# Sliding-window attention plus SwiGLU on one core: one edge mask and the normalisation reordered, and the feed-forward loop run across its chunk boundaries

## The chip, the cores and the metric

The kernel runs on one NeuronCore of a Trainium2 chip, written in Bass with every engine's instruction list and every semaphore wait laid out by hand. Times are device microseconds of one execution, from first to last instruction with what lies around them. The kernel before took 840.69 us, the median of six runs (839.28 to 843.67).

## The reference

One input x of 2048 tokens by 576 features in bf16 is normalised, and two branches are added to it:

```
xn  = layernorm(x)
q, k, v = heads(xn @ wqkv)                     # 32 heads of 18
p   = softmax(q k^T * 18**-0.5, masked to 0 <= query - key < 256)
out = x + (p v) @ wo + (silu(xn @ w1) * (xn @ w3)) @ w2     # F = 4608
```

## The kernel before

Every operation goes through a recorder, `R.emit(engine, ...)`, which appends it to that engine's list; each list then runs strictly in the order in which it was recorded. Waits are on counting semaphores, one per engine, so a wait for a later instruction of an engine covers all earlier ones. Where an instruction stands in its engine's list is therefore the whole schedule.

**Prologue.** Layernorm, transposes to `xnT`, and the Q, K and V projections.

**Attention** (lines 484 to 648). Heads go in 8 groups `g` of four, and the 2048 keys in 16 blocks `i` of 128, which gives 128 steps. In a step the four heads' scores of key block `i` against query blocks `i` to `i+2` (L532, 128 by 384 per head; the last two steps of a group have only 256 and 128 columns) lie in the four banks of the PSUM tensor `STB`, one bank a head. Heads 0 and 1 are pair `p = 0`, heads 2 and 3 are pair `p = 1`. For each pair ScalarE takes the exponential of two banks in one instruction (L569); VectorE multiplies the diagonal block by a 0/1 mask (L574, "diagonal mask"); GpSimd zeroes part of the third block with an `affine_select` (L579, "edge mask"), which only the step two later reads; and the next step's scores for the pair are put in TensorE's list, since the exponential has freed the banks. Then TensorE's list gets 12 small matmuls of probabilities with V (L605, "PV"), which wait for all masks of the step, and VectorE's list a copy of the result to bf16 (L619). Last comes `pend_ufin`, the end of the step before: a transpose on TensorE (L627) and, on VectorE, the reciprocal of the row sums (L630) and the multiplication by it (L633), both reading the transpose.

So TensorE's order is: scores of step i+1 for pair 0, for pair 1, PV of i, transpose of i-1, scores of i+2. VectorE's order is: two diagonal masks of i, copy of i, reciprocal and multiplication of i-1, two diagonal masks of i+1.

**Output projection** (lines 660 to 741) multiplies by `wo` and adds x, into `xatt`.

**Feed-forward** (lines 743 to 878). Four chunks `ci` of 512 tokens, each with 36 units `fi` of 128 hidden features, 144 units in all. A unit is ten matmuls for gate and up (L784 to L794, into three rotating banks `GU`), a tanh and a scaled copy on ScalarE (L803, L806), one VectorE operation (`gs`, L810), one GpSimd product (`hT`, L816), and then the W2 stage: five matmuls (L829, L832) that accumulate over the 36 units of the chunk in five PSUM banks. The W2 stage of a unit is recorded after the gate and up matmuls of the next unit, so that the chain through ScalarE, VectorE and GpSimd lies beside TensorE's work. At the end of a chunk, however, the loop `while pending_w2` (L843) records the last W2 stage at once, ahead of the next chunk's first matmuls. The read-out of a finished chunk is recorded after the next chunk's first gate and up matmuls and ahead of that unit's own ScalarE and VectorE operations: a ScalarE copy of the 128 leftover columns (L851), four transposes (L856), and for each of four token blocks two VectorE additions, of 448 and of 128 columns (L865, L867), both waiting for the transposes, and the output DMA (L871). Weights stream in through three slots, refilled by SyncE after a slot's last W2 stage.

Of the kernel before, what the change touches and what calls it, by code (L numbers as in the profile page):

```python
# [6 lines left out]
ACT = mybir.ActivationFunctionType  # L7
ALU = mybir.AluOpType
# [96 lines left out]
def bass_parallel_sum__sliding_block__glu_gated_swiglu__prompt_kernel(  # L105
# [35 lines left out]
    with ExitStack() as es:  # L141
# [380 lines left out]
        pend_ufin = None  # L522

        def rec_scores(g, i, hh):
            j = g % 2
            nq = min(3, NT - i)
            N = 128 * nq
            q0 = i * 128
            wl = [tok_rep[g], pair_free[hh // 2]]
            if g == 0 and i == 0:  # L530
                wl.append(last_prologue_pe)
            tsc = R.emit(PE, lambda e, hh=hh, j=j, q0=q0, N=N: e.matmul(  # L532
                STB[:, hh, 0:N], kT[j][32 * hh:32 * hh + Dh, q0:q0 + 128], qT[j][32 * hh:32 * hh + Dh, q0:q0 + N],
                tile_position=(32 * hh, 0)),
                waits=wl, sig=s_pe)
            scores_tok[(g, i, hh)] = tsc

        first_sc_wait = [t for t in qk_ring_free if t is not None]
        for hh in range(4):
# [4 lines left out]
                STB[:, hh, 0:N], kT[0][32 * hh:32 * hh + Dh, 0:128], qT[0][32 * hh:32 * hh + Dh, 0:N],  # L544
# [8 lines left out]
        for g in range(G):  # L553
            j = g % 2
            for i in range(NT):
# [3 lines left out]
                for p in range(2):  # L559
# [18 lines left out]
                    if nq == 3:  # L578
                        tem = R.emit(POOL, lambda e, ps0=ps0: e.affine_select(  # L579
                            out=pview[:, ps0:ps0 + 2, 2, :], in_=pview[:, ps0:ps0 + 2, 2, :],  # L580
                            compare_op=ALU.is_ge, fill=0.0,
                            base=-1, pattern=[[0, 2], [-1, 128]], channel_multiplier=1),
                            waits=[ta], sig=s_pool)
                        last_pool_tok = tem
                        toks.append(tem)
# [6 lines left out]
                    step_masks += toks  # L592
                ub = UB[:, i % 2, :]
# [22 lines left out]
                last_pe_tok = pv_last  # L616
                uj = u_ctr % 2
# [7 lines left out]
                def ufin(uj=uj, td=td, i=i, g=g):  # L625
                    nonlocal utp_free, pb6_free
# [17 lines left out]
            if g + 2 < G:  # L644
                repack(g + 2)
        if pend_ufin is not None:
            pend_ufin()
            pend_ufin = None

# [100 lines left out]
        k_ctr = 0  # L750
        pending_w2 = []
# [10 lines left out]
        pending_readout = None  # L762
        for ci, (t0b, ntb) in enumerate(TCH):
            N = 128 * ntb
            c0 = t0b * 128
            for fi in range(NF):
                fc = fi // 4
                fl = fi % 4
                n = ci * NFC + fc
                t1, t3, t2, sl = tok_wfill[n]  # L770
                k = k_ctr
                k_ctr += 1
                mg = (2 * k) % 3
                mu = (2 * k + 1) % 3
                kj = k % 2
                k3 = k % 3
                wlg = [t1, tok_xnT_all, gu_bank_free[mg]]
                wlu = [t3, tok_xnT_all, gu_bank_free[mu]]
                if first_ffn:
                    extra = [attn_act_last, attn_dve_last, ep_dve_last, ep_pe_last]  # L780
                    wlg += extra
                    wlu += extra
                for kd in range(4):
                    R.emit(PE, lambda e, mg=mg, sl=sl, kd=kd, fl=fl, c0=c0, N=N: e.matmul(  # L784
                        GU[mg][:, 0:N], W1c[sl][:, kd, fl * 128:(fl + 1) * 128], xnT[:, kd, c0:c0 + N],
                        start=(kd == 0), stop=False), waits=wlg)
                for kd in range(4):
                    R.emit(PE, lambda e, mu=mu, sl=sl, kd=kd, fl=fl, c0=c0, N=N: e.matmul(  # L788
                        GU[mu][:, 0:N], W3c[sl][:, kd, fl * 128:(fl + 1) * 128], xnT[:, kd, c0:c0 + N],
                        start=(kd == 0), stop=False), waits=wlu)  # L790
                tg = R.emit(PE, lambda e, mg=mg, sl=sl, fl=fl, c0=c0, N=N: e.matmul(  # L791
                    GU[mg][:, 0:N], W1c[sl][0:64, 4, fl * 128:(fl + 1) * 128], xnT[0:64, 4, c0:c0 + N],
                    start=False, stop=True), waits=wlg, sig=s_pe)
                tu = R.emit(PE, lambda e, mu=mu, sl=sl, fl=fl, c0=c0, N=N: e.matmul(  # L794
                    GU[mu][:, 0:N], W3c[sl][64:128, 4, fl * 128:(fl + 1) * 128], xnT[64:128, 4, c0:c0 + N],
                    start=False, stop=True, tile_position=(64, 0)), waits=wlu, sig=s_pe)
                first_ffn = False
                if fi == 0 and pending_readout is not None:
                    pending_readout()
                    pending_readout = None  # L800
                if pending_w2:
                    pending_w2.pop(0)()
                ta = R.emit(ACTE, lambda e, kj=kj, mg=mg, N=N: e.activation(  # L803
                    th[kj][:, 0:N], GU[mg][:, 0:N], ACT.Tanh, scale=0.5),
                    waits=[tg, th_free[kj]], sig=s_act)
                tb_ = R.emit(ACTE, lambda e, kj=kj, mu=mu, N=N: e.activation(  # L806
                    us[kj][:, 0:N], GU[mu][:, 0:N], ACT.Copy, scale=0.5),
                    waits=[tu, us_free[kj]], sig=s_act)
                gu_bank_free[mu] = tb_
                tdg = R.emit(DVE, lambda e, kj=kj, mg=mg, N=N: e.scalar_tensor_tensor(  # L810
                    out=gs[kj][:, 0:N], in0=th[kj][:, 0:N], scalar=1.0, in1=GU[mg][:, 0:N],
                    op0=ALU.add, op1=ALU.mult),
                    waits=[ta, gs_free[kj]], sig=s_dve)
                gu_bank_free[mg] = tdg
                th_free[kj] = tdg
                to = R.emit(POOL, lambda e, k3=k3, kj=kj, N=N: e.tensor_tensor(  # L816
                    hT[k3][:, 0:N], gs[kj][:, 0:N], us[kj][:, 0:N], ALU.mult),
                    waits=[tdg, tb_, hT_free[k3]], sig=s_pool)
                us_free[kj] = to
                gs_free[kj] = to  # L820

                def w2_stage(fi=fi, k3=k3, sl=sl, fl=fl, ntb=ntb, to=to, t2=t2, ci=ci, N=N):
                    wl = [to, t2]
                    if fi == 0:
                        wl.append(out_free)
                        if ci == 0:
                            wl += [attn_dve_last, attn_pe_last, attn_act_last, ep_dve_last, ep_pe_last]
                    for tbi in range(ntb):
                        R.emit(PE, lambda e, tbi=tbi, k3=k3, sl=sl, fl=fl: e.matmul(  # L829
                            OUT448[tbi][:, 0:DR], hT[k3][:, tbi * 128:(tbi + 1) * 128], W2c[sl][:, fl, 0:DR],  # L830
                            start=(fi == 0), stop=(fi == NF - 1)), waits=wl)
                    last = R.emit(PE, lambda e, k3=k3, sl=sl, fl=fl, N=N: e.matmul(  # L832
                        PB7[:, 0:N], W2c[sl][:, fl, DR:576], hT[k3][:, 0:N],
                        start=(fi == 0), stop=(fi == NF - 1)), waits=wl, sig=s_pe)
                    hT_free[k3] = last
                    if fl == 3:
                        wslot_free[sl] = last
                        issue_next_fill()
                    return last

                pending_w2.append(w2_stage)

            while pending_w2:  # L843
                pending_w2.pop(0)()
            last_pe = hT_free[(k_ctr - 1) % 3]

            def readout(last_pe=last_pe, ntb=ntb, t0b=t0b, N=N):
                nonlocal o64_ctr, ofin_ctr, out_free
                ojt = o64_ctr % 2
                o64_ctr += 1  # L850
                tcp = R.emit(ACTE, lambda e, ojt=ojt, N=N: e.activation(  # L851
                    o128[ojt][:, 0:N], PB7[:, 0:N], ACT.Copy),
                    waits=[last_pe, o64_free[ojt]], sig=s_act)
                ttp = None
                for tbi in range(ntb):
                    ttp = R.emit(PE, lambda e, tbi=tbi, ojt=ojt: e.transpose(  # L856
                        o128t[:, tbi, :], o128[ojt][:, tbi * 128:(tbi + 1) * 128], ident[:]),
                        waits=[tcp, tok_ident], sig=(s_pe if tbi == ntb - 1 else None))
# [58 lines left out]
```

## Time and profile before

| what | value |
|---|---|
| median of six runs | 840.69 us (839.28 to 843.67) |
| the profiled execution: its time, its span | 840.42 us, 838.7 us |
| mean granted TensorE clock over the span | 0.852 |
| busy: TensorE, VectorE, ScalarE, GpSimd | 750.8, 325.0, 366.4, 273.5 us |
| attention, first score matmul to last normalisation | 93.3 to 323.1 us |
| feed-forward, first gate matmul to last W2 matmul | 362.3 to 832.5 us |

Busy time is the share in which an engine had an instruction running; TensorE's ends are modelled, and so its busy time is not a measure of how full it is. [...]

### The profile page before, as it was taken

Reading aid. Unit: us, or ns where it says so; the run is one execution under the profiler, and the core shown is the slowest. Engines: PE = TensorE matmul, PEld = TensorE weight load, DVE = VectorE, ACT = ScalarE, POOL = GpSimd, SP = SyncE. Lnnn points to the kernel's source line nnn. Section 1 sums busy time; section 2 is a strip of 40 time slices with the busy share of each in tenths; the row PEclk is TensorE's granted clock in tenths of the full one; section 3 lists DMA queues with packets and bytes.
Section 4 is the critical chain, followed back from the end, with each engine's and each line's share of the span. In section 5 each row is a group of like instructions: output and inputs, shape, how many; then the busy total and the mean of one; then the engine's idle time right before and its main releaser. Section 6 shows DMA issues by size and latency. Waiting matters only on the chain. (4 is left out here: it accounts for less than half of the span.)

```text
span 838.7 us, 13024 instructions
## 1 busy us (share of the span) xinstructions
PE 750.8 (90%) x4906; PEld 309.6 (37%) x4952; DVE 325.0 (39%) x974; ACT 366.4 (44%) x601; POOL 273.5 (33%) x410
## 2 busy tenths in 40 slices
PE   4999878777887788999999899999899999899996
PEld 2455323222222223434444334444344443344442
DVE  5564466666666664532222222222212222222222
ACT  1233678777877781023333333333233333233332
POOL 2111234333433340023333233333233333233332
PEclk9999755555555555999999999999999999999998
DMA  6110200110111006505445444454434534354320
GB/s 183 29 29 1 57 10 21 30 29 5 26 30 29 2 1 185 170 15 169 121 133 170 133 149 124 131 170 131 152 104 152 166 115 144 113 169 142 115 83 28
DMA packets 73917, 78.99 MB, mean 94 GB/s; under 512 B 4352, under 2 KB 72704, under 8 KB 73856
## 3 DMA queue, kind: packets, MB, share of 16 engines
q1 hardware_dynamic: 71552, 75.81, 30.4%
q10 hardware_dynamic: 2304, 2.36, 1.0%
q8 instruction: 39, 0.64, 0.3%
q14 instruction: 22, 0.18, 0.1%
HBM read 71.07 MB, written 2.36 MB: 88 GB/s over the span
## 5 line engine op out<-in xcount | busy, mean ns | idle before, releaser
L816 POOL TENSOR_TENSOR hT<-gs,us 128x512 bf16<-128x512 bf16 x144 | 165.7, 1151 | 348.2 <-DVE gs L810 348.2
L803 ACT ACTIVATE th<-stb 128x512 bf16<-128x512 f32 x144 | 86.0, 597 | 344.1 <-PE stb L794 344.1
L810 DVE SCALAR_TENSOR_TENSOR gs<-th,stb 128x512 bf16<-128x512 bf16 x144 | 99.0, 687 | 346.3 <-ACT th L803 346.3
L569 ACT ACTIVATE area<-stb 128x768 bf16<-128x768 f32 (+2 forms) x256 | 183.1, 768 | 42.5 <-PE stb L532 41.3
L788 PE MATMUL stb<-xnT,area 128*128 128x512 bf16 x555 | 144.3, 379 | 9.2 <-DVE gs L810 8.1
L784 PE MATMUL stb<-xnT,area 128*128 128x512 bf16 x573 | 148.5, 382 | 2.0 <-DVE xatt L728 1.0
L579 POOL TENSOR_SCALAR_AFFINE_SELECT area<-area 128x256 bf16<-128x256 bf16 x224 | 93.1, 416 | 151.4 <-ACT area L569 151.4
L605 PE MATMUL ub<-area 128*20 128x128 bf16 x1440 | 61.7, 301 | 45.4 <-DVE area L574 44.8
L532 PE MATMUL stb<-qT,kT 18*128 18x384 bf16 (+1 forms) x508 | 100.0, 475 | 1.4 <-ACT area L569 1.3
L806 ACT ACTIVATE us<-stb 128x512 bf16<-128x512 f32 x144 | 85.2, 592 | 0.0
L788 PEld LDWEIGHTS stb<-xnT,area 128*128 128x128 bf16 x576 | 56.1, 98 | 77.6 <-DVE gs L810 10.1
L784 PEld LDWEIGHTS stb<-xnT,area 128*128 128x128 bf16 x576 | 56.5, 99 | 65.6 <-issue 2.9
L574 DVE TENSOR_TENSOR area<-area,mask 128x256 bf16<-128x256 bf16 x256 | 78.0, 343 | 2.5 <-ACT area L569 2.5
L829 PE MATMUL ub<-area,hT 128*128 128x448 bf16 x288 | 78.7, 355 | 0.0
L619 DVE CAST uTsb<-ub 128x128 bf16<-128x128 f32 x128 | 37.4, 292 | 76.0 <-PE ub L605 76.0
L605 PEld LDWEIGHTS ub<-area 128*20 128x20 bf16 x1440 | 27.3, 109 | 93.5 <-DVE area L574 93.5
L829 PE MATMUL stb<-area,hT 128*128 128x448 bf16 x144 | 52.4, 364 | 6.4 <-POOL hT L816 6.4
L794 PE MATMUL stb<-xnT,area 64*128 64x512 bf16 x144 | 55.8, 388 | 0.0
L791 PE MATMUL stb<-xnT,area 64*128 64x512 bf16 x144 | 55.8, 388 | 0.0
L829 PE MATMUL pb<-area,hT 128*128 128x448 bf16 x144 | 51.2, 356 | 0.0
L832 PE MATMUL pb<-hT,area 128*128 128x512 bf16 x126 | 48.3, 383 | 0.0
L532 PEld LDWEIGHTS stb<-qT,kT 18*128 18x128 bf16 x508 | 24.8, 99 | 43.8 <-ACT area L569 29.1
(71 smaller groups left out, 533.5 us busy)
## 6 DMA issues: line engine op xcount, KB each, us to landing
area<-in_B_w_dram SPq DMA_DIRECT2D x72, 512.0 KB, 4.5
area<-in_B_w_dram SPq DMA_DIRECT2D x36, 576.0 KB, 6.1
area<-in_B_w_dram SPq DMA_DIRECT2D x72, 64.0 KB, 4.8
xin<-in_A_x_dram SPq DMA_DIRECT2D x16, 144.0 KB, 2.1
qT<-QTu SPq DMA_DIRECT2D x32, 72.0 KB
kT<-KTu SPq DMA_DIRECT2D x32, 72.0 KB
xres<-in_A_x_dram ACTq DMA_DIRECT2D x16, 144.0 KB, 2.3
out_dram<-ofin SPq DMA_DIRECT2D x16, 144.0 KB, 5.5
```

Source lines behind the costliest of these rows:

```text
L532: tsc = R.emit(PE, lambda e, hh=hh, j=j, q0=q0, N=N: e.matmul(STB[:, hh, 0:N], kT[j][32 * hh:32 * hh + Dh, q0:q0 + 128], qT[j][32 * hh:32 ...
L569: ta = R.emit(ACTE, lambda e, ps0=ps0, p=p, N=N: e.activation(pT3[:, ps0:ps0 + 2, 0:N], STB[:, 2 * p:2 * p + 2, 0:N], ACT.Exp, scale=scale ...
L574: tdm = R.emit(DVE, lambda e, ps0=ps0: e.tensor_tensor(pview[:, ps0:ps0 + 2, 0, :], pview[:, ps0:ps0 + 2, 0, :], mask_diag_b, ALU.mult), w ...
L579: tem = R.emit(POOL, lambda e, ps0=ps0: e.affine_select(out=pview[:, ps0:ps0 + 2, 2, :], in_=pview[:, ps0:ps0 + 2, 2, :], compare_op=ALU.i ...
L605: t_ = R.emit(PE, lambda e, hh=hh, ub=ub, kb=kb, g=g, ps=ps, jx=jx, start=start, stop=stop: e.matmul(ub[32 * hh:32 * hh + VW, 0:128], Vaug ...
L784: R.emit(PE, lambda e, mg=mg, sl=sl, kd=kd, fl=fl, c0=c0, N=N: e.matmul(GU[mg][:, 0:N], W1c[sl][:, kd, fl * 128:(fl + 1) * 128], xnT[:, kd ...
L788: R.emit(PE, lambda e, mu=mu, sl=sl, kd=kd, fl=fl, c0=c0, N=N: e.matmul(GU[mu][:, 0:N], W3c[sl][:, kd, fl * 128:(fl + 1) * 128], xnT[:, kd ...
L803: ta = R.emit(ACTE, lambda e, kj=kj, mg=mg, N=N: e.activation(th[kj][:, 0:N], GU[mg][:, 0:N], ACT.Tanh, scale=0.5), waits=[tg, th_free[kj] ...
L806: tb_ = R.emit(ACTE, lambda e, kj=kj, mu=mu, N=N: e.activation(us[kj][:, 0:N], GU[mu][:, 0:N], ACT.Copy, scale=0.5), waits=[tu, us_free[kj ...
L810: tdg = R.emit(DVE, lambda e, kj=kj, mg=mg, N=N: e.scalar_tensor_tensor(out=gs[kj][:, 0:N], in0=th[kj][:, 0:N], scalar=1.0, in1=GU[mg][:, ...
L816: to = R.emit(POOL, lambda e, k3=k3, kj=kj, N=N: e.tensor_tensor(hT[k3][:, 0:N], gs[kj][:, 0:N], us[kj][:, 0:N], ALU.mult), waits=[tdg, tb ...
L829: R.emit(PE, lambda e, tbi=tbi, k3=k3, sl=sl, fl=fl: e.matmul(OUT448[tbi][:, 0:DR], hT[k3][:, tbi * 128:(tbi + 1) * 128], W2c[sl][:, fl, 0 ...
```

## The change

Four edits, in attention and in the feed-forward loop.

1. Pair 0 now uses banks 2 and 3 of `STB`, and pair 1 banks 0 and 1.
2. Pair 1's edge mask is a VectorE multiplication by the mask (as the diagonal mask is), recorded after the step's PV and no longer among what that PV waits for; the later PVs that read the block wait for it. Pair 0's stays on GpSimd.
3. The end of a step is cut in two. The transpose stays where it was; the reciprocal and the multiplication (`norm`) are recorded one step later, after that step's diagonal masks and before its PV.
4. The feed-forward loop runs over all 144 units in one sequence. The last W2 stage of a chunk comes after the next chunk's first gate and up matmuls, as every other W2 stage does, and the read-out after that unit's own ScalarE, VectorE and GpSimd operations. In the read-out the four 448-column additions come first and wait only for the W2 stage, and the four 128-column additions follow them and wait for the transposes.

```diff
-                STB[:, hh, 0:N], kT[j]...
+                STB[:, (hh + 2) % 4, 0:N], kT[j]...
...
-                        pT3[:, ps0:ps0 + 2, 0:N], STB[:, 2 * p:2 * p + 2, 0:N], ACT.Exp, scale=scale),
+                        pT3[:, ps0:ps0 + 2, 0:N], STB[:, 2 - 2 * p:4 - 2 * p, 0:N], ACT.Exp, scale=scale),
...
                     if nq == 3:
-                        tem = R.emit(POOL, lambda e, ps0=ps0: e.affine_select(
...
+                        if p == 0:
+                            tem = R.emit(POOL, lambda e, ps0=ps0: e.affine_select(
...
+                        else:
+                            late_edge = (ps0, ta)
...
                     step_masks += toks
+                if pend_norm is not None:
+                    pend_norm()
+                    pend_norm = None
...
                 last_pe_tok = pv_last
+                if nq == 3:
+                    ps0, ta = late_edge
+                    tem = R.emit(DVE, lambda e, ps0=ps0: e.tensor_tensor(
+                        pview[:, ps0:ps0 + 2, 2, :], pview[:, ps0:ps0 + 2, 2, :], mask_edge_b, ALU.mult),
+                        waits=[ta], sig=s_dve)
+                    for hh in (2, 3):
+                        mask_tok[(g, i, hh)] = mask_tok[(g, i, hh)] + [tem]
...
                     uT_free[uj] = tp
+                    pend_norm = lambda: norm(tp, uj, i, g)
+
+                def norm(tp, uj, i, g):
+                    nonlocal utp_free, pb6_free
                     tr = R.emit(DVE, lambda e: e.reciprocal(
```

The feed-forward loop after the change, with what did not change cut out:

```
for k, (ci, fi) in enumerate(units):
    ...                                  # ten gate and up matmuls
    last_w2 = None
    if prev is not None:
        last_w2 = rec_w2(prev)           # five W2 matmuls of the unit before
    ...                                  # tanh, copy, gs, hT of this unit
    if prev is not None and fi == 0:
        pci = prev[7]
        rec_readout(last_w2, TCH[pci][1], TCH[pci][0], 128 * TCH[pci][1])
    prev = (fi, k3, sl, fl, ntb, to, t2, ci, N)
last_w2 = rec_w2(prev)
rec_readout(last_w2, TCH[-1][1], TCH[-1][0], 128 * TCH[-1][1])
```

## Rows read from the trace of the kernel before

**Rows 1.** Busy time by stretch (us, instructions), granted clock, DMA share, GB/s.

```profile
200.00:250.00 50.00, 39.82 (x454) 14.25 (x452) 32.63 (x142) 40.17 (x57) 20.11 (x49) 0.50 0.10 25
602.00:604.00 2.00, 2.00 (x8) 0.83 (x7) 0.69 (x1) 1.09 (x2) 0.55 (x1) 0.50 0.77 270
```

**Rows 2.** Timeline of one attention step: start, length, engine, line; idle before, releaser.

```profile
98.50 1.51 ACT L569 ACTIVATE area<-stb 128x768 bf16<-128x768 f32 x2 [0.33 <-PE stb L532]
99.04 0.50 PE L605 MATMUL ub<-area 128*20 128x128 bf16 x12 [0.32 <-DVE area L574]
...
99.48 0.29 PE L627 MATMUL pb<-ident,uTsb 128*128 128x128 bf16 x1
99.59 0.29 DVE L619 CAST uTsb<-ub 128x128 bf16<-128x128 f32 x1 [0.61 <-PE ub L605]
...
99.70 0.87 PE L532 MATMUL stb<-qT,kT 18*128 18x384 bf16 x4
99.80 0.18 DVE L630 RECIPROCAL rden<-pb 128x4 f32<-128x4 bf16 x1
100.02 0.23 DVE L633 TENSOR_TENSOR O_all<-pb,rden 128x72 bf16<-128x72 bf16 x1
...
100.08 0.41 POOL L579 TENSOR_SCALAR_AFFINE_SELECT area<-area 128x256 bf16<-128x256 bf16 x1 [0.29 <-ACT area L569]
100.17 0.66 DVE L574 TENSOR_TENSOR area<-area,mask 128x256 bf16<-128x256 bf16 x2
100.26 1.51 ACT L569 ACTIVATE area<-stb 128x768 bf16<-128x768 f32 x2 [0.26 <-PE stb L532]
...
100.88 0.50 PE L605 MATMUL ub<-area 128*20 128x128 bf16 x12 [0.32 <-DVE area L574]
```

**Rows 3.** Timeline of ScalarE: the first and the last two tanh.

```profile
364.55 0.60 ACT L803 ACTIVATE th<-stb 128x512 bf16<-128x512 f32 x1 [45.17 <-PE stb L794]
...
825.57 0.60 ACT L803 ACTIVATE th<-stb 128x512 bf16<-128x512 f32 x1 [2.04 <-PE stb L794]
...
828.70 0.60 ACT L803 ACTIVATE th<-stb 128x512 bf16<-128x512 f32 x1 [2.04 <-PE stb L794]
```

**Rows 4.** Timeline across the last chunk boundary.

```profile
712.36 0.36 PE L829 MATMUL stb<-area,hT 128*128 128x448 bf16 x1 [1.77 <-POOL hT L816]
...
713.34 1.03 PE L784 MATMUL stb<-xnT,area 128*128 128x512 bf16 x4
...
713.54 0.60 ACT L851 ACTIVATE o<-pb 128x512 bf16<-128x512 f32 x1 [2.70 <-PE pb L832]
...
715.49 0.40 PE L856 MATMUL pb<-ident,o 128*128 128x128 bf16 x4
...
715.72 1.03 PE L784 MATMUL stb<-xnT,area 128*128 128x512 bf16 x4
...
715.92 0.62 DVE L865 TENSOR_TENSOR ofin<-stb,xatt 128x448 bf16<-128x448 f32 x1 [4.84 <-PE pb L856]
...
716.46 0.21 DVE L867 TENSOR_TENSOR ofin<-pb,xatt 128x128 bf16<-128x128 bf16 x1
716.59 0.62 DVE L865 TENSOR_TENSOR ofin<-ub,xatt 128x448 bf16<-128x448 f32 x1
...
719.32 1.04 PE L788 MATMUL stb<-xnT,area 128*128 128x512 bf16 x4 [2.57 <-DVE gs L810]
```

**Rows 5.** Timeline: exponentials back to back; masks without GpSimd beside them.

```profile
93.72 4.45 ACT L569 ACTIVATE area<-stb 128x768 bf16<-128x768 f32 x6
...
318.84 0.48 DVE L574 TENSOR_TENSOR area<-area,mask 128x256 bf16<-128x256 bf16 x2
```

**Rows 6.** Diagonal masks at 150 to 250 us: least, median and greatest ns.

```profile
L574 DVE TENSOR_TENSOR area<-area,mask x114: 277/283/492, 150.1 to 249.8; 128x256 bf16<-128x256 bf16 x114
```

**Rows 7.** Timeline of the end, and of the first four input DMAs.

```profile
831.30 0.36 PE L829 MATMUL stb<-area,hT 128*128 128x448 bf16 x1 [1.56 <-POOL hT L816]
...
834.36 2.32 SPq L871 DMA_DIRECT2D out_dram<-ofin  x4
...
0.79 1.81 SPq L264 DMA_DIRECT2D xin<-in_A_x_dram  x4
```

More of the change, by code (lines that the diff above doesn't have):

```diff
@@ L532, in rec_scores @@
             tsc = R.emit(PE, lambda e, hh=hh, j=j, q0=q0, N=N: e.matmul(
-                STB[:, hh, 0:N], kT[j][32 * hh:32 * hh + Dh, q0:q0 + 128], qT[j][32 * hh:32 * hh + Dh, q0:q0 + N],
+                STB[:, (hh + 2) % 4, 0:N], kT[j][32 * hh:32 * hh + Dh, q0:q0 + 128], qT[j][32 * hh:32 * hh + Dh, q0:q0 + N],
                 tile_position=(32 * hh, 0)),
@@ L578, in bass_parallel_sum__sliding_block__glu_gated_swiglu__prompt_kernel @@
                     if nq == 3:
-                        tem = R.emit(POOL, lambda e, ps0=ps0: e.affine_select(
[L580 to L585, printed above, removed]
+                        if p == 0:
+                            tem = R.emit(POOL, lambda e, ps0=ps0: e.affine_select(
+                                out=pview[:, ps0:ps0 + 2, 2, :], in_=pview[:, ps0:ps0 + 2, 2, :],
+                                compare_op=ALU.is_ge, fill=0.0,
+                                base=-1, pattern=[[0, 2], [-1, 128]], channel_multiplier=1),
+                                waits=[ta], sig=s_pool)
+                            last_pool_tok = tem
+                            toks.append(tem)
+                        else:
+                            late_edge = (ps0, ta)
                     for hh in (2 * p, 2 * p + 1):
@@ L592, in bass_parallel_sum__sliding_block__glu_gated_swiglu__prompt_kernel @@
                     step_masks += toks
+                if pend_norm is not None:
+                    pend_norm()
+                    pend_norm = None
                 ub = UB[:, i % 2, :]
@@ L625, in ufin @@
                 def ufin(uj=uj, td=td, i=i, g=g):
-                    nonlocal utp_free, pb6_free
+                    nonlocal pend_norm
                     tp = R.emit(PE, lambda e: e.transpose(utp, uT_sb[uj][:], ident[:]),
@@ L645, in bass_parallel_sum__sliding_block__glu_gated_swiglu__prompt_kernel @@
                 repack(g + 2)
+        if pend_norm is not None:
+            pend_norm()
         if pend_ufin is not None:
@@ L648, in bass_parallel_sum__sliding_block__glu_gated_swiglu__prompt_kernel @@
             pend_ufin = None
+            pend_norm()
         attn_dve_last = tok_O[(G - 1, NT - 1)]
@@ L749, in bass_parallel_sum__sliding_block__glu_gated_swiglu__prompt_kernel @@
         ofin_ctr = 0
-        k_ctr = 0
-        pending_w2 = []
         o64_ctr = 0
@@ L761, in bass_parallel_sum__sliding_block__glu_gated_swiglu__prompt_kernel, with rec_w2 @@
         first_ffn = True
-        pending_readout = None
-        for ci, (t0b, ntb) in enumerate(TCH):
+        units = [(ci, fi) for ci in range(len(TCH)) for fi in range(NF)]
+        prev = None
+        def rec_w2(info):
+            (fi, k3, sl, fl, ntb, to, t2, ci, N) = info
+            wl = [to, t2]
+            if fi == 0:
+                wl.append(out_free)
+                if ci == 0:
+                    wl += [attn_dve_last, attn_pe_last, attn_act_last, ep_dve_last, ep_pe_last]
+            for tbi in range(ntb):
+                R.emit(PE, lambda e, tbi=tbi: e.matmul(
+                    OUT448[tbi][:, 0:DR], hT[k3][:, tbi * 128:(tbi + 1) * 128], W2c[sl][:, fl, 0:DR],
+                    start=(fi == 0), stop=(fi == NF - 1)), waits=wl)
+            last = R.emit(PE, lambda e: e.matmul(
+                PB7[:, 0:N], W2c[sl][:, fl, DR:576], hT[k3][:, 0:N],
+                start=(fi == 0), stop=(fi == NF - 1)), waits=wl, sig=s_pe)
+            hT_free[k3] = last
+            if fl == 3:
+                wslot_free[sl] = last
+                issue_next_fill()
+            return last
@@ new lines, in rec_readout @@
+        def rec_readout(last_pe, ntb, t0b, N):
+            nonlocal o64_ctr, ofin_ctr, out_free
+            ojt = o64_ctr % 2
+            o64_ctr += 1
+            tcp = R.emit(ACTE, lambda e: e.activation(
+                o128[ojt][:, 0:N], PB7[:, 0:N], ACT.Copy),
+                waits=[last_pe, o64_free[ojt]], sig=s_act)
+            ttp = None
+            for tbi in range(ntb):
+                ttp = R.emit(PE, lambda e, tbi=tbi: e.transpose(
+                    o128t[:, tbi, :], o128[ojt][:, tbi * 128:(tbi + 1) * 128], ident[:]),
+                    waits=[tcp, tok_ident], sig=(s_pe if tbi == ntb - 1 else None))
+            o64_free[ojt] = ttp
+            ojs = []
+            for tbi in range(ntb):
+                oj = ofin_ctr % NOF
+                ofin_ctr += 1
+                ojs.append(oj)
+                tblk = t0b + tbi
+                R.emit(DVE, lambda e, oj=oj, tbi=tbi, tblk=tblk: e.tensor_tensor(
+                    ofin[oj][:, 0:DR], OUT448[tbi][:, 0:DR], xatt[:, tblk, 0:DR], ALU.add),
+                    waits=[last_pe, tok_xatt[tblk], (s_out[oj], s_out[oj].count)])
+            for tbi in range(ntb):
+                oj = ojs[tbi]
+                tblk = t0b + tbi
+                tdo = R.emit(DVE, lambda e, oj=oj, tbi=tbi, tblk=tblk: e.tensor_tensor(
+                    ofin[oj][:, DR:576], o128t[:, tbi, :], xatt[:, tblk, DR:576], ALU.add),
+                    waits=[ttp, tok_xatt[tblk]], sig=s_dve)
+                out_free = tdo
+                R.emit(SP, lambda e, oj=oj, tblk=tblk: e.dma_start(out2[tblk * 128:(tblk + 1) * 128, :], ofin[oj][:]),
+                       waits=[tdo], sig=s_out[oj], amount=16)
@@ L764, in bass_parallel_sum__sliding_block__glu_gated_swiglu__prompt_kernel @@
+        for k, (ci, fi) in enumerate(units):
+            t0b, ntb = TCH[ci]
             N = 128 * ntb
             c0 = t0b * 128
[L766 to L858, printed above, removed]
-                o64_free[ojt] = ttp
-                for tbi in range(ntb):
-                    oj = ofin_ctr % NOF
-                    ofin_ctr += 1
-                    tblk = t0b + tbi
-                    wl = [last_pe, ttp, tok_xatt[tblk], (s_out[oj], s_out[oj].count)]
-                    R.emit(DVE, lambda e, oj=oj, tbi=tbi, tblk=tblk: e.tensor_tensor(
-                        ofin[oj][:, 0:DR], OUT448[tbi][:, 0:DR], xatt[:, tblk, 0:DR], ALU.add), waits=wl)
-                    tdo = R.emit(DVE, lambda e, oj=oj, tbi=tbi, tblk=tblk: e.tensor_tensor(
-                        ofin[oj][:, DR:576], o128t[:, tbi, :], xatt[:, tblk, DR:576], ALU.add),
-                        waits=wl, sig=s_dve)
-                    out_free = tdo
-                    R.emit(SP, lambda e, oj=oj, tblk=tblk: e.dma_start(out2[tblk * 128:(tblk + 1) * 128, :], ofin[oj][:]),
-                           waits=[tdo], sig=s_out[oj], amount=16)
@@ L875, in bass_parallel_sum__sliding_block__glu_gated_swiglu__prompt_kernel @@
-            pending_readout = readout
-        if pending_readout is not None:
-            pending_readout()
-            pending_readout = None
+            fc = fi // 4
+            fl = fi % 4
+            n = ci * NFC + fc
+            t1, t3, t2, sl = tok_wfill[n]
+            mg = (2 * k) % 3
+            mu = (2 * k + 1) % 3
+            kj = k % 2
+            k3 = k % 3
+            wlg = [t1, tok_xnT_all, gu_bank_free[mg]]
+            wlu = [t3, tok_xnT_all, gu_bank_free[mu]]
+            if first_ffn:
+                extra = [attn_act_last, attn_dve_last, ep_dve_last, ep_pe_last]
+                wlg += extra
+                wlu += extra
@@ new lines, in bass_parallel_sum__sliding_block__glu_gated_swiglu__prompt_kernel @@
+            for kd in range(4):
+                R.emit(PE, lambda e, mg=mg, sl=sl, kd=kd, fl=fl, c0=c0, N=N: e.matmul(
+                    GU[mg][:, 0:N], W1c[sl][:, kd, fl * 128:(fl + 1) * 128], xnT[:, kd, c0:c0 + N],
+                    start=(kd == 0), stop=False), waits=wlg)
+            for kd in range(4):
+                R.emit(PE, lambda e, mu=mu, sl=sl, kd=kd, fl=fl, c0=c0, N=N: e.matmul(
+                    GU[mu][:, 0:N], W3c[sl][:, kd, fl * 128:(fl + 1) * 128], xnT[:, kd, c0:c0 + N],
+                    start=(kd == 0), stop=False), waits=wlu)
@@ new lines, in bass_parallel_sum__sliding_block__glu_gated_swiglu__prompt_kernel @@
+            tg = R.emit(PE, lambda e, mg=mg, sl=sl, fl=fl, c0=c0, N=N: e.matmul(
+                GU[mg][:, 0:N], W1c[sl][0:64, 4, fl * 128:(fl + 1) * 128], xnT[0:64, 4, c0:c0 + N],
+                start=False, stop=True), waits=wlg, sig=s_pe)
+            tu = R.emit(PE, lambda e, mu=mu, sl=sl, fl=fl, c0=c0, N=N: e.matmul(
+                GU[mu][:, 0:N], W3c[sl][64:128, 4, fl * 128:(fl + 1) * 128], xnT[64:128, 4, c0:c0 + N],
+                start=False, stop=True, tile_position=(64, 0)), waits=wlu, sig=s_pe)
@@ new lines, in bass_parallel_sum__sliding_block__glu_gated_swiglu__prompt_kernel @@
+            first_ffn = False
+            last_w2 = None
+            if prev is not None:
+                last_w2 = rec_w2(prev)
+            ta = R.emit(ACTE, lambda e, kj=kj, mg=mg, N=N: e.activation(
+                th[kj][:, 0:N], GU[mg][:, 0:N], ACT.Tanh, scale=0.5),
+                waits=[tg, th_free[kj]], sig=s_act)
+            tb_ = R.emit(ACTE, lambda e, kj=kj, mu=mu, N=N: e.activation(
+                us[kj][:, 0:N], GU[mu][:, 0:N], ACT.Copy, scale=0.5),
+                waits=[tu, us_free[kj]], sig=s_act)
@@ new lines, in bass_parallel_sum__sliding_block__glu_gated_swiglu__prompt_kernel @@
+            gu_bank_free[mu] = tb_
+            tdg = R.emit(DVE, lambda e, kj=kj, mg=mg, N=N: e.scalar_tensor_tensor(
+                out=gs[kj][:, 0:N], in0=th[kj][:, 0:N], scalar=1.0, in1=GU[mg][:, 0:N],
+                op0=ALU.add, op1=ALU.mult),
+                waits=[ta, gs_free[kj]], sig=s_dve)
+            gu_bank_free[mg] = tdg
+            th_free[kj] = tdg
+            to = R.emit(POOL, lambda e, k3=k3, kj=kj, N=N: e.tensor_tensor(
+                hT[k3][:, 0:N], gs[kj][:, 0:N], us[kj][:, 0:N], ALU.mult),
+                waits=[tdg, tb_, hT_free[k3]], sig=s_pool)
@@ L880, in bass_parallel_sum__sliding_block__glu_gated_swiglu__prompt_kernel @@
+            us_free[kj] = to
+            gs_free[kj] = to
+            if prev is not None and fi == 0:
[4 more added lines that the diff above has]
+        rec_readout(last_w2, TCH[-1][1], TCH[-1][0], 128 * TCH[-1][1])
         fin = [(so, so.count) for so in s_out]
```

2 lines of the change are left out of this document (1 added, 1 removed).

## The prediction

> **What bounds the kernel now.** I read the busy times by stretch first, then the timeline of one attention step, then the timeline across a chunk boundary. The reader is to see that the two halves have different limits.
>
> [...] What sets the step is a ring, and there are two that close at the same length. The first goes through VectorE: PV starts at 99.04, the copy of its result 0.55 later, the multiplication 0.43 after that, the diagonal masks 0.15 later, both done after 0.66, and the next PV 0.05 on, at 100.88 [rows 2]. That is 1.84; the exponentials of the same two steps start 1.76 apart, the step alternates, and the mean is 1.80. The second goes through ScalarE and takes two steps: the exponentials end at 98.50 + 1.51 = 100.01; the PV that needs them starts 0.87 later, the transpose 0.44 after PV, the scores 0.22 after the transpose, the exponentials 0.56 after the scores, and these last 1.51 [rows 2]. The sum, 3.60, is 1.80 a step. Both rings share the 0.87, in which the diagonal masks stand in VectorE's list behind the copy, the reciprocal and the multiplication of an older block. ScalarE and TensorE each sit idle for about 0.3 of every step on account of it [rows 2].
>
> In the feed-forward part the bound is TensorE: units follow each other at 828.70 - 825.57 = 3.13 [rows 3]. The 143 intervals from the first tanh to the last should take 143 x 3.13 = 447.6 and took 464.15, so 16.6 us are lost at the three chunk boundaries [rows 3]. At the one shown TensorE waits 1.77 for the last hidden block and then 2.57 because the VectorE operation that frees a bank stands behind eight additions [rows 4]. After such a boundary the granted clock falls to 0.50 for a short stretch [rows 1].
>
> **The change, part by part.**
>
> *Bank rotation.* The same waits on the same pairs with other bank numbers: no instruction more, no instruction moved, and TensorE writes one pair of banks while ScalarE reads the other, as before. I cost it at nothing, and see no reason for a gain or a loss.
>
> *Normalisation one step later, and pair 1's edge mask on VectorE.* These go together. VectorE's order becomes: masks of i, reciprocal and multiplication of i-2, edge mask of i, copy of i. The reciprocal and multiplication (starts 0.43 after the copy, 0.15 before the next operation [rows 2]) now run while PV runs. So the time from the end of the exponentials to PV shrinks to release, mask, release: 0.07 from ScalarE to the operation that waits for it (GpSimd's start at 100.08), 0.28 for a mask alone (two in 0.48, the second starting 0.20 after the first [rows 5]), 0.05 to PV: 0.40. TensorE has a floor of its own, since the scores of pair 1 stand ahead of PV and start when the exponentials end; the four score matmuls end by the model at 99.70 + 0.87 = 100.57, which is 0.56 after the exponentials [rows 2], but their tail overlaps what follows. The bounds are 0.40 and 0.56, and I take 0.44, nearer the mask's row, because the modelled end is late. The second ring is then 0.44 + 0.44 + 0.22 + 0.56 + 1.51 = 3.17, or 1.585 a step, a gain of 0.215; over 128 steps 27.5 us. At 0.40 it is 30 us, at 0.56 it is 20 us.
>
> What the ring leaves behind must fit. VectorE's share of a step is, by starts, two masks 0.40, reciprocal 0.22, multiplication 0.15, edge mask 0.20, copy 0.21: 1.2 of 1.585 [rows 2, 5]. The added mask is covered by PV's run: the copy could not start before PV's start + 0.55 anyway. The transpose of i-1 now waits for the multiplication of i-2, which stands behind the masks of i: 0.35 + 0.22 + 0.23 + 0.06 = 0.86 after the exponentials, against 0.44 + 0.44 = 0.88 for PV to clear TensorE. That wait is level with what it stands beside, and it is the next thing late. GpSimd loses a 0.41 operation a step that nobody will miss. ScalarE's floor is (4.45 - 1.51) / 4 = 0.735 an exponential, 1.47 a step [rows 5]: no longer far away.
>
> A mask's length is not one number: 277 to 492 ns with a median of 283 [rows 6], and the pair at 100.17 took 0.66 with GpSimd running beside it against 0.48 without [rows 2, 5]. [...]
>
> *The feed-forward loop.* At a boundary the two waits of 1.77 and 2.57 go [rows 4]: the last W2 stage has a unit's matmuls ahead of it, and the bank-freeing operation stands ahead of the additions. What is late next is TensorE itself: the transposes stand in its list behind W2 and wait for the ScalarE copy. The copy starts 1.18 after W2's first matmul (713.54 - 712.36), takes 0.60, and with 0.05 for the release the transposes start at 1.83; they hold TensorE 0.23 (715.49 to 715.72), so the next gate matmul starts at 2.06 where it would start at 0.98 (713.34 - 712.36) [rows 4]. The cost is 1.08 a boundary, 3.2 for three. Behind them the first W2 stage of the new chunk waits for all eight additions: four of 0.54 and four of 0.13 [rows 4], from 1.2 to 1.4 after W2 began to at most 4.1; TensorE gets there after ten more matmuls, 2.14 (713.34 to 715.48), at 4.20. No wait, with little to spare; if it slips, it costs up to 1 us a boundary. SyncE's output DMAs stand behind a refill issued earlier, as before. With one gap of about 0.85 in place of 1.77 and 2.57 I expect no fall of the clock. The gain is 16.6 - 3.2 = 13.4; bounds 10 and 14.
>
> *The end.* The last W2 stage still waits for its own chain. The 448-column additions can start 1.18 after it begins, at 832.5, and the last 128-column one ends near 835; but the four output DMAs are issued one after another, and four took 1.81 at the start of the kernel [rows 7]. From about 834.9 that ends at 836.7, where it ended before (834.36 + 2.32). I count 0, between -0.3 and +0.3.
>
> **Sum.** 840.4 (the profiled execution; the median of the runs is 0.3 above it) - 27.5 - 13.4 = 799.5 us. With the bounds of each part together: 796 to 811.
>
> **Rivals.**
> 1. *The wait moves to the transpose.* If the deferred multiplication comes late, the transpose holds up the scores and attention gains nothing. For that it must end 0.45 later than reckoned, since the transpose started 0.87 + 0.44 = 1.31 after the exponentials before. For it: it now stands behind two masks and is level already. Against: both masks at their greatest row, 0.49 each, add only 0.4. Time: 840.4 - 13.4 = 827. Half of it would give 813.
> [...]
> 3. *VectorE becomes the bound, and slower.* If its operations don't overlap and all three masks run at the greatest length, a step is 3 x 0.49 + 0.18 + 0.23 + 0.29 = 2.17 [rows 2, 6], 0.37 above now: 840.4 + 47 - 13.4 = 874. The kernel is slower from 1.80 + 13.4/128 = 1.90 a step on. Against: starts follow each other at 0.20 to 0.22 in the rows, and one GpSimd operation in place of two leaves less to collide with.
>
> **How the numbers follow.** Forecast 0.76, rival 1 in whole or half 0.10, rival 2 0.10, rival 3 0.04. The range 783 to 815 holds the forecast, most of rival 2 and the half case of rival 1. About 0.3%, 2.5 us, is what a measurement of this kernel can tell from no change. Slower is rival 3, 0.04; the same needs the gains of one half eaten by the other, 0.02; faster 0.94.
>
> **What would show it.** In the changed profile: exponentials of successive steps about 1.58 apart; PV starting 0.40 to 0.56 after the exponentials end, with the reciprocal and multiplication beside PV; the copy no longer ahead of waiting masks; ScalarE's idle time in attention under 0.1 a step. At the boundaries: one TensorE gap of about 0.85 that ScalarE's copy ends, none ended by GpSimd or by `gs`, and 464.15 - 13.4 = 451 us from first tanh to last. A step still at 1.80, or a granted clock above 0.50 in attention, makes the prediction wrong.

## The result

The changed kernel takes 800.32 us, the median of eight runs (799.32 to 804.25), against 840.54 for the kernel before: a ratio of 0.9526 (95% interval 0.9509 to 0.9543). The forecast was 799.5. The profiled execution took 799.7 us with a span of 797.9, so 40.8 us of span went. They can be placed by the starts of the stages:

| stage | before | after | gain |
|---|---|---|---|
| to the first score matmul | 93.31 | 93.72 | -0.4 |
| attention, to the end of the last normalisation | 93.31 to 323.08 | 93.72 to 296.79 | 26.7 |
| output projection and first unit, to the first tanh | to 364.55 | to 337.66 | 0.6 |
| first to last tanh | 464.15 | 450.01 | 14.1 |
| last tanh to the end | 10.0 | 10.2 | -0.2 |

Busy time of the changed kernel in the same 50 us of attention as in [rows 1] (columns: TensorE, its weight loads, VectorE, ScalarE, GpSimd, granted clock, DMA):

```profile
200.00:250.00 50.00, 47.26 (x520) 16.46 (x519) 41.79 (x188) 45.47 (x65) 11.47 (x29) 0.50 0.10 25
```

TensorE went from 39.82 to 47.26 busy, ScalarE from 40.17 to 45.47, GpSimd from 20.11 to 11.47, and the granted clock, a share of TensorE's full speed, stayed at 0.50. One attention step of the changed kernel, the rows that answer to [rows 2]:

```profile
199.66 0.80 ACT L570 ACTIVATE area<-stb 128x768 bf16<-128x768 f32 x1
...
200.20 0.58 DVE L575 TENSOR_TENSOR area<-area,mask 128x256 bf16<-128x256 bf16 x2
200.51 0.10 PEld L533 LDWEIGHTS stb<-qT,kT 18*128 18x128 bf16 x2 [0.32 <-ACT area L570]
200.66 3.02 ACT L570 ACTIVATE area<-stb 128x768 bf16<-128x768 f32 x4 [0.20 <-PE stb L533]
200.70 0.18 DVE L648 RECIPROCAL rden<-pb 128x4 f32<-128x4 bf16 x1
200.91 0.23 DVE L651 TENSOR_TENSOR O_all<-pb,rden 128x72 bf16<-128x72 bf16 x1
...
200.94 0.50 PE L612 MATMUL ub<-area 128*20 128x128 bf16 x12
201.06 0.28 DVE L626 TENSOR_TENSOR area<-area,mask 128x256 bf16<-128x256 bf16 x1
...
201.38 0.29 PE L641 MATMUL pb<-ident,uTsb 128*128 128x128 bf16 x1
201.50 0.29 DVE L633 CAST uTsb<-ub 128x128 bf16<-128x128 f32 x1 [0.16 <-PE ub L612]
...
201.60 1.13 PE L533 MATMUL stb<-qT,kT 18*128 18x384 bf16 x4
...
203.88 2.32 ACT L570 ACTIVATE area<-stb 128x768 bf16<-128x768 f32 x3 [0.20 <-PE stb L533]
```

Four exponentials now run back to back, 3.02 long, and the next four begin 3.22 after the first began: 1.61 a step in place of 1.80; ScalarE's one wait in the two steps is 0.20, which is 0.10 a step. The exponentials end at 199.66 + 0.80 = 200.46 and PV starts at 200.94, 0.48 later instead of 0.87. Reciprocal and multiplication lie beside PV, and the copy at 201.50 waits 0.16 for PV instead of 0.61. The masks are done at 200.78, before PV starts; what ends just ahead of PV is pair 1's scores, whose weights were loaded at 200.51.

The first and the last two tanh answer to [rows 3]:

```profile
337.66 0.60 ACT L872 ACTIVATE th<-stb 128x512 bf16<-128x512 f32 x1 [43.85 <-PE stb L865]
...
784.54 0.60 ACT L872 ACTIVATE th<-stb 128x512 bf16<-128x512 f32 x1 [2.04 <-PE stb L865]
...
787.67 0.60 ACT L872 ACTIVATE th<-stb 128x512 bf16<-128x512 f32 x1 [2.04 <-PE stb L865]
```

A unit still takes 3.13. The first chunk boundary, beside [rows 4]:

```profile
449.76 0.36 PE L792 MATMUL stb<-area,hT 128*128 128x448 bf16 x1
...
450.94 0.60 ACT L808 ACTIVATE o<-pb 128x512 bf16<-128x512 f32 x1
451.09 0.62 DVE L823 TENSOR_TENSOR ofin<-stb,xatt 128x448 bf16<-128x448 f32 x1
...
451.59 0.40 PE L813 MATMUL pb<-ident,o 128*128 128x128 bf16 x4 [0.69 <-ACT o L808]
451.83 1.03 PE L855 MATMUL stb<-xnT,area 128*128 128x512 bf16 x4
...
453.22 0.61 DVE L829 TENSOR_TENSOR ofin<-pb,xatt 128x128 bf16<-128x128 bf16 x4
...
453.98 0.36 PE L792 MATMUL stb<-area,hT 128*128 128x448 bf16 x1
```

The waits of 1.77 and 2.57 are gone. One is left, which ScalarE's copy ends, and the next gate matmul starts 2.07 after W2's first. The additions end at 453.83, 0.15 before TensorE wants the banks. At the end of the kernel, beside [rows 7]:

```profile
790.28 0.36 PE L792 MATMUL stb<-area,hT 128*128 128x448 bf16 x1 [1.56 <-POOL hT L885]
...
793.60 0.60 DVE L829 TENSOR_TENSOR ofin<-pb,xatt 128x128 bf16<-128x128 bf16 x4
793.84 1.82 SPq L833 DMA_DIRECT2D out_dram<-ofin  x4
```

The last four output DMAs are issued 1.82 long, from 3.56 to 5.38 after the last W2 stage began; before they ran from 3.06 to 5.38, each behind its own block's additions, of which the last ended 5.01 after that stage began (at 836.31). Now the last addition ends after 3.92, the issues follow each other, and nothing ends sooner.

### The profile page after: what moved, and what is told of

It reads as the page before. It is cut to its first block, busy times and chain, and to the rows that moved or that the text cites. A ratio compares the mean times of both kernels' runs of the same rounds, so it can differ in the third digit from the quotient of the medians.

```text
span 797.9 us, 13024 instructions
## 1 busy us (share of the span) xinstructions
PE 753.8 (94%) x4906; PEld 309.7 (39%) x4952; DVE 344.6 (43%) x1086; ACT 365.6 (46%) x601; POOL 226.9 (28%) x298
## 4 chain that ended last, share of the span: by engine, by line
PE 80%; ACT 12%; DVE 3%; DMA 3%; issue 2%; SPq 1%; POOL 0%; DVEq 0%; ACTq 0%
PE stb L855 16%; PE stb L859 15%; ACT area L570 11%; PE stb L533 7%; PE ub L792 7%; PE stb L862 6%; PE stb L792 5%; PE stb L380 4%; PE ub L612 4%; PE pb L792 3%; PE pb L795 3%; PE ub L339 2%; PE pb L641 2%; DMA xres<-in_A_x_dram 2%; PE ub L732 1%
## 5 line engine op out<-in xcount | busy, mean ns | idle before, releaser
L533 PE MATMUL stb<-qT,kT 18*128 18x384 bf16 (+1 forms) x508 | 114.5, 476 | 9.7 <-ACT area L570 3.1
L581 POOL TENSOR_SCALAR_AFFINE_SELECT area<-area 128x256 bf16<-128x256 bf16 x112 | 46.4, 414 | 171.9 <-ACT area L570 171.9
```

## The experiments

**The halves apart.** The attention edits alone, and the feed-forward loop alone:

```diff
 e1: attention of the changed kernel, feed-forward loop (L743 to L878) of the kernel before
 e2: attention of the kernel before, feed-forward loop of the changed kernel
```

> The attention edits with the feed-forward loop of before. Theory (the two halves have separate limits and their gains add): the attention part loses 26.7 us as in the changed kernel, the feed-forward part takes its 464 us as before, 814 us. Rival (the halves interact, for instance the earlier start of the weight stream costs or gives something later): the loss from before lies outside 25 to 29 us.

> The new feed-forward loop with the attention of before. Theory: first tanh to last tanh takes 450.0 us as in the changed kernel, against 464.2, and the rest is unchanged: 826.5 us. Rival (halves interact): outside 824.5 to 828.5.

The first took 817.05 us, ratio 0.97 (0.9674 to 0.9726), a gain of 24.3, just outside what was expected. Its profiled execution took 813.6, with 202.99 in attention and 464.06 from the first tanh to the last, which are the theory's numbers; the three timed runs took 817 at a granted clock of 0.862 against 0.866. Where those 3.4 us lie is open, since only one execution has a trace. The traces show two things that differ between executions. One is how often the clock falls from 1.00 to 0.50 at the old boundaries: at one of three in e3 (below), at two here and in the kernel before (there at 602 to 604 us [rows 1] and at 722 to 724), at three in e4, with 462.47, 464.06, 464.15 and 465.48 from the first tanh to the last, so a fall goes with about 1.5 us more, an estimate from these four. The other is when the clock comes back after attention (last section). The second took 825.86, ratio 0.9815 (0.9797 to 0.9834), with 450.02 between the tanh. The two gains, 24.3 and 15.5, add to 39.8; together the edits gave 40.2.

**The two attention edits apart**, each in the kernel before:

```diff
 e3 (late normalisation alone)
...
+                    pend_norm = lambda: norm(tp, uj, i, g)
 e4 (pair 1's edge mask alone)
-                        toks.append(tem)          # GpSimd, both pairs
...
+                        else:
+                            late_edge = (ps0, ta) # VectorE, after PV
...
+                    norm(tp, uj, i, g)            # at once, as before
```

> Only the late normalisation, all else of before; both edge masks stay on GpSimd and in what PV waits for. Theory (a step is the longer of two rings): the VectorE ring is opened, but PV now waits for GpSimd's mask of pair 1 and for a VectorE mask that collides with it, about 0.67 us after the exponentials in place of 0.87: 1.70 us a step, 828 us (824 to 832). Rival 1 (the order of the normalisation is the whole gain): 814. Rival 2 (relieving GpSimd is the whole gain): 840.

> Only pair 1's edge mask on VectorE, after PV; the normalisation stays directly behind the copy. Theory: the VectorE ring stays closed (PV, copy, reciprocal, multiplication, two masks) and gains only what the masks lose in length when GpSimd is not beside them, 0.04 to 0.14 us a step: 822 to 835, 829. Rival 1 (the order of the normalisation is the whole gain): 840. Rival 2 (relieving GpSimd is the whole gain): 814.

The late normalisation alone took 828.19 us, ratio 0.9848 (0.9824 to 0.9872). One of its steps:

```profile
211.73 3.02 ACT L570 ACTIVATE area<-stb 128x768 bf16<-128x768 f32 x4 [0.46 <-PE stb L533]
...
214.74 0.69 DVE L575 TENSOR_TENSOR area<-area,mask 128x256 bf16<-128x256 bf16 x2
214.82 0.47 POOL L581 TENSOR_SCALAR_AFFINE_SELECT area<-area 128x256 bf16<-128x256 bf16 x1 [0.30 <-ACT area L570]
...
215.20 3.02 ACT L570 ACTIVATE area<-stb 128x768 bf16<-128x768 f32 x4 [0.45 <-PE stb L533]
...
215.48 0.50 PE L610 MATMUL ub<-area 128*20 128x128 bf16 x12 [0.18 <-DVE area L575]
```

The exponentials end at 214.75, GpSimd starts its edge mask at once, the two VectorE masks take 0.69 beside it, and PV starts 0.73 after the exponentials. Four exponentials start 3.47 after the four before them, 1.73 a step. The edge mask alone took 825.17 us, ratio 0.9807 (0.9779 to 0.9835):

```profile
212.80 1.51 ACT L570 ACTIVATE area<-stb 128x768 bf16<-128x768 f32 x2 [0.15 <-PE stb L533]
...
213.24 0.50 PE L612 MATMUL ub<-area 128*20 128x128 bf16 x12
...
213.79 0.29 DVE L633 CAST uTsb<-ub 128x128 bf16<-128x128 f32 x1 [0.41 <-PE ub L612]
...
214.22 0.23 DVE L650 TENSOR_TENSOR O_all<-pb,rden 128x72 bf16<-128x72 bf16 x1
214.37 0.48 DVE L575 TENSOR_TENSOR area<-area,mask 128x256 bf16<-128x256 bf16 x2
...
214.91 0.50 PE L612 MATMUL ub<-area 128*20 128x128 bf16 x12
```

This is the ring of the kernel before, with the same 0.55, 0.43 and 0.15 in it [rows 2]. Only the pair of masks has shrunk, to 0.48, and PV follows PV after 1.67. That is 0.13 less than the mean of 1.80, and 0.13 x 128 = 16.6 us. PV starts 0.60 after the exponentials end at 214.31.

So neither edit is the whole gain. How far the two add is read from attention alone, because the runs' 13.1 and 16.2 also hold what differs in the feed-forward loop, where neither edit is. From the first score to the last normalisation the traces take 229.77 before, 217.49 with e3, 214.22 with e4 and 203.07 with both: 12.3 and 15.6, together 27.8, against 26.7. The gains add but for about 1 us, and two traces of the old attention (before and e2) differ by 0.4. Each edit takes its own part of the same stretch, the 0.87 from the exponentials to PV: 0.14 with the first, 0.27 with the second, 0.39 with both.

**What holds PV in the changed kernel.** Pair 1's diagonal mask is left out of the computation, and PV waits for the exponential in its place:

```diff
-                    tdm = R.emit(DVE, ... mask_diag_b, ALU.mult), waits=[ta], sig=s_dve)
+                    tdm = ta
+                    if p == 0:
+                        tdm = R.emit(DVE, ... mask_diag_b, ALU.mult), waits=[ta], sig=s_dve)
```

> The changed kernel without pair 1's diagonal mask (left out, so those probabilities are unmasked), PV waiting for the exponential itself. Theory (in the changed kernel PV is held by TensorE's own list, where pair 1's scores stand ahead of it): PV still starts about 0.46 us after the exponentials, step 1.60, 799 us (796 to 802). Rival (PV is held by the mask, 0.07 + 0.28 + 0.05): PV starts up to 0.35 earlier, ScalarE's floor of 1.47 to 1.51 decides, 785 to 789.

It took 798.83 us, ratio 0.9514 (0.9475 to 0.9552), no different from the changed kernel by its interval. A step of it, with the weight loads of pair 1's scores and of PV:

```profile
209.28 0.10 PEld L533 LDWEIGHTS stb<-qT,kT 18*128 18x128 bf16 x2 [0.35 <-ACT area L570]
...
209.72 0.50 PE L614 MATMUL ub<-area 128*20 128x128 bf16 x12
```

PV starts 0.44 after the scores' weights, as in the changed kernel (200.51 to 200.94, 0.43). In the wide steps the mask was not what held it; TensorE's own list was. At a group's end, where the scores are narrower, the mask does count: attention takes 200.96 in this trace against 203.07, and most of the 2.1 lies there.

**Scores ahead of the transpose.** In TensorE's list the transpose of an older block goes behind pair 0's next scores:

```diff
+                    if p == 0 and len(pend_list) >= 2:
+                        pend_list.pop(0)()        # transpose of i-1, behind the scores of i+2
...
-                if pend_ufin is not None:
-                    pend_ufin()
```

> The changed kernel with the transpose of an older block put behind pair 0's next scores in TensorE's list in place of ahead of them. Theory (the two-step ring through ScalarE decides, 0.47 + 0.44 + 0.22 + 0.57 + 1.51 = 3.21): without the 0.22 it is 2.99, and the floor is ScalarE's 1.47 to 1.51 or TensorE's 0.43 + 0.43 + 0.44 + 0.22 = 1.52 a step; 1.52 is 789 us (787 to 793). Rival (VectorE's list sets the step): 800.

It took 790.33 us, ratio 0.9402 (0.9369 to 0.9435). TensorE's list over one step:

```profile
219.78 0.50 PE L533 MATMUL stb<-qT,kT 18*128 18x384 bf16 x2
...
220.21 0.29 PE L640 MATMUL pb<-ident,uTsb 128*128 128x128 bf16 x1
...
220.42 0.50 PE L533 MATMUL stb<-qT,kT 18*128 18x384 bf16 x2
...
220.86 0.50 PE L614 MATMUL ub<-area 128*20 128x128 bf16 x12
...
221.29 0.50 PE L533 MATMUL stb<-qT,kT 18*128 18x384 bf16 x2
```

Busy time in 100 us of attention, columns as in the first such row:

```profile
150.00:250.00 100.00, 99.09 (x1097) 35.28 (x1093) 84.96 (x396) 96.49 (x135) 24.28 (x60) 0.50 0.11 26
```

Starts follow each other at 0.43, 0.21, 0.44 and 0.43, together 1.51 a step: TensorE's list at the clock that it is granted is now full, and ScalarE is 0.96 busy beside it. The ring through ScalarE was what was left in the changed kernel, and shortening it by the transpose gave 10 us.

**The bank rotation** undone in the changed kernel:

```diff
-                STB[:, (hh + 2) % 4, 0:N], ...
+                STB[:, hh, 0:N], ...
```

> The changed kernel with the banks of the score pairs as before. Theory: the rotation costs and gives nothing, 800.3 us, within 2.5. Rival (which banks a pair has matters, at the seams with the prologue or the output projection or in every step): outside 797.8 to 802.8.

It took 801.64 us (799.05 to 803.38), ratio 0.9529 (0.9495 to 0.9563). That is the changed kernel's ratio; an effect above some 3 us is excluded. In the traces attention takes 203.00 without the rotation and 203.07 with it.

**The boundary.** First the read-out's transposes and late additions one unit later, then the other way, the 448-column additions waiting for the transposes as in the kernel before, both in the changed kernel:

```diff
 e8
...
-                rec_readout(last_w2, ...)
+                pend_rest = rec_readout(last_w2, ...)   # copy and 448-column additions now,
...
+            if pend_rest is not None:                   # the rest after the next ten matmuls
+                pend_rest()
 e10
-                    waits=[last_pe, tok_xatt[tblk], ...])
+                    waits=[last_pe, ttp, tok_xatt[tblk], ...])
```

> The changed kernel with the four read-out transposes and the 128-column additions recorded one unit later, behind the next ten gate and up matmuls, and the first W2 stage of a chunk waiting for the 448-column additions alone except in its last matmul. Theory (a boundary still costs TensorE a wait of 0.7 to 0.85 for the ScalarE copy): that goes at three boundaries, 2.1 to 2.6 less, 798 us. Rival (the wait comes back as the last W2 matmul waiting for the late additions): 800 or more.

> The changed kernel with the 448-column additions waiting for the transposes too. Theory (at a boundary the additions end only about 0.1 us before the first W2 stage of the new chunk needs their banks): started 0.9 later they hold that stage up by 0.8, three times, and the output DMAs of the end start about 1 us later: 803.5 us (802 to 805). Rival (the additions have room and are hidden either way): 800.3.

> The changed kernel again, on the same chip as the two beside it, as their reference: 800.3 us, within 1.5. A time outside that would mean that chips differ by more than the small steps that these two are to show.

The first took 798.6 us (797.91 to 799.16), ratio 0.9495 (0.9469 to 0.9521), 1.7 below the changed kernel's median, in the direction expected but within the interval. The trace shows it more sharply: 448.41 from the first tanh to the last against 450.01, 1.6 less where 2.1 to 2.6 was expected. The wait is gone and a short one is in its place:

```profile
452.73 0.40 PE L829 MATMUL pb<-ident,o 128*128 128x128 bf16 x4
...
453.30 0.35 PE L796 MATMUL stb<-area,hT 128*128 128x448 bf16 x1 [0.17 <-DVE ofin L821]
```

The second took 803.87 us, ratio 0.9568 (0.9548 to 0.9588), with the changed kernel at 799.73, ratio 0.9515 (0.9496 to 0.9535), on the same chip: 4.1 slower, where 3.2 was expected. The first W2 stage of the new chunk now waits:

```profile
455.37 0.35 PE L792 MATMUL stb<-area,hT 128*128 128x448 bf16 x1 [0.88 <-DVE ofin L829]
```

**Both improvements together**, e7 and e8 in one kernel:

> The changed kernel with pair 0's next scores ahead of the transpose and the read-out's transposes one unit later, together. Theory (the two save in different stretches and add): 790.3 - 2 = 788.5 us (787 to 790). Rival (one gives back what the other saves): 790 or more.

It took 788.39 us (788.12 to 788.57), ratio 0.9382 (0.9363 to 0.9402), beside 799.73 for the changed kernel on that chip. It is faster than the kernel before and than the changed kernel.

## Why the prediction was right

*The two rings.* The step was forecast from the right stretch, but that two rings closed at the same length was a wrong reading. In a steady schedule the start-to-start times around any loop add up to whole steps, so the 3.60 of the second ring is twice 1.80 whatever holds it, and its 0.87 contains a wait. Before, the two diagonal masks started at 100.17, 0.15 behind the multiplication, although the exponentials had let GpSimd's edge mask start at 100.08 [rows 2]: they waited for VectorE's list. The ring through VectorE held the step, and the one through ScalarE had room. Had both been equally long, and each edit shortened one, neither would have gained alone. With the normalisation out of the way (e3) the step is 1.73, with the diagonal masks and GpSimd's edge mask side by side (0.69) ahead of PV; with the masks shortened (e4) VectorE's ring closes at 1.67; with both, PV waits only for TensorE's own list.

What the sum had right is what it kept fixed. From PV to the transpose, the scores and the exponentials the traces show the same 0.44, 0.22, 0.56 and 1.51, within 0.01, before, with e3, with e4 and after. So a step loses half of what the 0.87 loses: at 0.73 it is 1.73, at 0.60 it is 1.67, at 0.48 it is 1.61.

*From the exponentials to PV.* I took 0.44 between bounds of 0.40 and 0.56; it is 0.48, 0.05 to the weights of pair 1's scores and 0.43 from there to PV. I put the 0.44 near the mask's row, because the modelled end of the scores was late; the floor in the wide steps was TensorE's after all, since PV stayed where it was without the mask. The size was nearly right with the weight on the wrong one of the two floors.

*From a step to 128.* That attention gave 26.7 us for 27.5 is in part luck. The wide steps gave less than the 0.215 reckoned: in group 3 the first exponentials of step 0 and of step 13 start at 178.60 and 201.72 before, at 169.33 and 189.98 after, which is 0.19 a step. From there to the next group's first, at 207.00 and 194.40, it is 0.29 a step. The narrow steps at a group's end, counted like the others, made up for a part of it.

*The masks' length.* With no GpSimd operation beside it the pair took 0.48 (e4), and 0.69 with one (e3). In the kernel before, the 110 diagonal masks that started while a GpSimd edge mask was running took 380 to 492 ns, and the 18 that started before one took 279 to 293. Why a mask is longer beside a GpSimd operation is not shown. Pair 1's diagonal mask, the one that the forecast rested on, took 281 to 294 in all 128 steps of the changed kernel.

*The transpose's wait.* Reckoned level with PV's end, it was not close: the multiplication ends at 201.14, the transpose starts at 201.38, 0.24 later, and PV to transpose is 0.44 as before. Rival 1 is out.

*The feed-forward loop.* The boundary cost was right, 2.07 for 2.06. The gain was 14.1 for 13.4, because the loss of the kernel before was mis-sized by rounding a unit to 3.13 and counting the first interval, which is 2.77 in both kernels, as a full one. The forecast that the clock would not fall was right as well: it stays at 1.00 at the boundaries in all nine traces with the new loop. By the 1.5 a fall, an estimate from the four traces of the old loop, the two falls in the kernel before are about 3 of its 464.15, so the gain depends on the execution: 12.5 against e3's 462.47 and 15.5 against e4's 465.48. The parts of the loop's edit (the late W2 stage, the later read-out, the order of the additions) were not tried apart, except for what the additions wait for. That the additions would be ready with little to spare (0.15) is shown by e10, in which 0.88 appeared as soon as they started late.

*The end.* Zero, as the issue of the output DMAs has it; measured -0.2.

*Rivals 2 and 3.* Rival 2, for which the range went down to 783, was the author's estimate of attention at a granted clock of 1.00. No run shows that clock in a denser attention: in the stretches read it is 0.50, with TensorE 0.95 busy in the changed kernel and 0.99 in e7. VectorE is 0.84 busy at 1.61 a step, so the loss of rival 3 did not come either. The bank rotation gave nothing that could be seen.

## What to carry to other kernels

When two engines are both idle in every step, look for a ring through their instruction lists and write down each link's start-to-start time. The sum alone proves nothing, since any loop of a steady schedule comes to whole steps: ask of each link whether it ends a wait, or whether the operation was released earlier and stood behind something else in its list. A stretch that two causes fill gives up a part to each edit (12.3 and 15.6 here, 26.7 together), until the next engine's list holds it. An in-order list often holds an old block's leftover work ahead of the one operation that others wait for: move the leftover behind it, into time in which that engine waits anyway. After the edit add up the list of each engine over a step, for the fullest list is the next floor, and moving one short operation in it behind the urgent one can be worth as much as a stall.

## What was not expected of the hardware

In the stretches of attention read, TensorE was granted the same clock however full its list was: 0.80 busy by the model before, 0.95 in the changed kernel and 0.99 in e7, each at 0.50. In the output projection the clock came back to 1.00, but not always equally soon. The same stretch in two executions of the changed kernel, that of the result and that of e11:

```profile
300.00:302.00 2.00, 2.00 (x15) 0.91 (x14) 0.00 (x0) 0.00 (x0) 0.00 (x0) 0.90 0.97 264
```

```profile
300.00:302.00 2.00, 2.00 (x10) 0.57 (x9) 0.00 (x0) 0.00 (x0) 0.00 (x0) 0.50 1.06 308
```

and a stretch of the kernel before:

```profile
330.00:332.00 2.00, 2.00 (x10) 0.60 (x9) 0.46 (x2) 0.00 (x0) 0.00 (x0) 0.56 1.10 353
```

A figure between 0.50 and 1.00 is a mean over a stretch in which the clock changed: the changed kernel's is 0.50 at 298 to 300 us, 0.90 at 300 to 302 and 1.00 at 302 to 304. It rose 3.6 us after the last normalisation in the first, 8.8 in the second and 8.7 in the kernel before, but 4.1 in e2, which has the attention of before, and 13.1 in e7. So the time of its return goes with the execution and not with this change, and the 0.6 us of the output projection in the table (41.47 against 40.87; 41.45 in e11) is not a gain of the change. What sets the time of the return is not shown.
